# Gating six sums of b and forming M's blocks during the second f pass, with accumulating stores into the output

## The chip, the cores and the metric

The kernel runs on one core of one Trainium2 chip. Each core has a matrix engine (TensorE, PE below; its weight loads are shown apart as PEld), a vector engine (VectorE, DVE), a scalar engine (ScalarE, ACT), GpSimd (POOL) and SyncE (SP). In this kernel POOL and SP issue transfers and compute nothing that matters here. SP's transfers go through a hardware queue (q1 in the profile), POOL's through a software queue (q0); both use the core's 16 DMA engines. The metric is the time of one execution on the device in microseconds.

## The reference

Two layers read the same input x (2048 tokens, width 640) and are mixed by a gate for each token:

```python
x = A_x
g = _sigmoid((x * gate_w).sum(-1, keepdims=True))
a = _A_ref(x, A_wqkv, A_wo)
b = _B_ref(x, B_w_gate, B_w_up, B_w_down)
return g * a + (1 - g) * b
```

`_A_ref` is a linear attention with 32 heads of 20: q, k and v come from one product with `wqkv`, `phi` makes q and k positive, `kv` and `z` are sums over all tokens, and the output is `num / den` times `wo`. `_B_ref` is a gated unit with 1536 hidden columns: `(sigmoid(x Wg) * (x Wu)) Wd`.

## The kernel before

**Data.** The output is held transposed, `out_t` with 640 rows (five blocks `o` of 128) and 2048 columns of tokens (four groups `g` of 512). A product of float32 values is made of three matmuls (`mm3`, lines 406 to 408): each operand is split into a high part (ACT copies, line 419) and a low part (DVE subtracts, line 423), and high x high, high x low and low x high are added up in PSUM.

**Fewer products.** Many block products are made by a scheme for 2 x 2 blocks with seven products in place of eight, which needs sums and differences of blocks ahead of the products.

**Order of the work.** After `kv` and `z`, the matrix M (`kv` of each head times `wo`, 640 x 640, stored as `m_dram`) takes the place of both in the attention: a = (phi(q) M) / den. The gated unit goes over the tokens in two pairs of groups: first groups 2 and 3 (`pr` = 1), then groups 0 and 1 (`pr` = 0, the second pair). In each pair a loop `f_phase` runs over 12 blocks f of hidden columns, in seven steps s; at odd f from 3 on, a generator `down_pair` multiplies two finished hidden blocks by their down weights and adds the results into the tile `tb` (five o, two g). The down weights are loaded in three pieces into `wf` by `load_wf` (SP's queue, line 363). After both pairs come the attention products of groups 2 and 3 (eleven units with (0, 4) behind; `a_unit`, n counts them), and those of groups 0 and 1 (two `ABlock`s and two single units).

**What b becomes.** In the first pair, the ten sums of `tb` are stored into `b_dram`. Six of them, (o, g) = (0..3, 1), (1, 0) and (3, 0), are stored once; the other four are stored in two goes, the second an accumulating store. For the attention units of groups 2 and 3 all ten are loaded back as `bl` (`load_b`), multiplied by `omg`, which is 1 - g for each token (`load_omg`, `scale_b`), and added to the product by DVE (`finish`), which then goes to `out_t`. From the fourth unit on the product of `bl` and `omg` is first written to the PSUM bank (`queue_seed`), and PE adds its product to this seed; ACT copies the result (line 419) and SP stores it.

**M's blocks.** In the second pair's f, `queue_m` loads the rows of M as `mr`, splits them into `mt` and stores them as `mp_dram`, for the units. For the 2 x 2 scheme of groups 0 and 1, sums and differences of M's blocks are needed as well: `load_ms` loads raw rows ahead of f = 11 on POOL's queue (`mt`, then `mr` and `mv`, 16 loads of 80 KB), and `queue_ms` makes the sums (DVE, in two parts) and the splits into weights between the units, at about 689 to 704 us.

**The denominator** runs on the side: `pden` loads are summed by DVE into `fac` (line 427), stored as `den_dram`, loaded again with another layout, inverted and stored as `fac_dram`; SP loads that as `fac`, the factor by which DVE scales phi(q) (`pq_scale`).

**What sets the order.** Each engine works in program order. The order of ACT's and DVE's side work is set by a planner (`Order`): `order.add` queues a piece with its costs, `order.fill` puts queued pieces where its own model of the engines sees room, `order.need` forces one. Waits between engines come from the data. SP and POOL each issue their transfers in order; a POOL transfer takes one of eight slots in turn and waits until the transfer that had the slot has landed.

Of the kernel before, what the change touches and what calls it, by code (L numbers as in the profile page):

```python
# [7 lines left out]
F32 = mybir.dt.float32  # L8
# [365 lines left out]
def gated_mix_kernel(ctx: ExitStack, tc: tile.TileContext, xt, xn, wk, wv, wo, wst_q, wst_f, out_t):  # L374
# [70 lines left out]
    def add(out, a, b, after=""):  # L445
        vec2(out, a, b, OP.add, after)
# [12 lines left out]
    b_dram = dram.tile([P, KC, 2, TG], F32, name="b_dram")  # L459
    mp_dram = dram.tile([P, KC, 2, D], F32, name="mp_dram")  # L460
    gate_dram = dram.tile([2, S], F32, name="gate_dram")
    gate_rep = dram.tile([S // P, H, P], F32, name="gate_rep")
# [1260 lines left out]
    def queue_m(u=0):  # L1723
# [13 lines left out]
        order.add(a_cost(D), v_cost(D), fn, "m", lambda: order.when(raw) + DEN_LAG / 2, spare=True)  # L1737

    def m_close():
        nonlocal tb  # L1740
        mp_cm.__exit__(None, None, None)
        m1_cm.__exit__(None, None, None)
        kp_cm.__exit__(None, None, None)
        down_pool.append(ctx.enter_context(tc.tile_pool(name="down", bufs=1, reuse_waits="tile")))
        down_cms.append(tc.tile_pool(name="down1", bufs=1, reuse_waits="tile"))
        down_pool.append(down_cms[0].__enter__())
        tb = down_pool[0].tile([P, KC, 2, TG], F32, name="tb")
        sp.t = max(sp.t, order.act + A_LAG, order.vec + V_LAG, gp.cell[0])
        load_d()
        load_d()  # L1750
        for n in waiting_d:
            queue_d(n)
        other.append(Next(0, 1, xf, CW, c1_x, True))
# [142 lines left out]
    seen = set()  # L1896

    class DownPair:

# [269 lines left out]
    def f_phase(pr, q, hooks={}):  # L2169
# [67 lines left out]
        for f in range(FC):  # L2237
# [5 lines left out]
            if f % 2 and f > 1:  # L2243
                if pr:
                    pass
                elif f == FC - 3:
# [3 lines left out]
                    load_ms(0)  # L2250
                    load_ms(1)
                elif f == FC - 1:
                    load_m(0)
                down = down_pair(pr, f // 2 - 1)
# [118 lines left out]
    order.slack(False)  # L2373
    q = q_phase(0, lambda k: [tuple(t[:, k] for t in b12)], {0: [lambda: next(down), more_c], 1: [lambda: next(down)], 8: [lambda: order.need((nx[1], 6), False)], 9: [lambda: queue_ds(LAST), lambda: queue_df(LAST)], 10: [lambda: queue_last("T2", "T3", "T4")]})

    groups = (2, 3, 0, 1)
    PL, PQ, BL, OMG, MHL = {}, {}, {}, {}, {}

# [32 lines left out]
    def load_b(g):  # L2411

        if g < 2:
            BL[g] = [tb[:, o, g] for o in range(KC)]
        elif g == groups[0]:
            BL[g] = [ct("bl") for _ in range(KC)]
            for o in reversed(range(KC)):
                sp.dma_start(BL[g][o], b_dram[:, o, g - 2])
        else:
            t = [x3_tile("bl") for _ in range(2)]  # L2420
            sp.dma_start(t[0], b_dram[:, 0:3, g - 2])
            sp.dma_start(t[1][:, 0:2], b_dram[:, 3:5, g - 2])
            BL[g] = [t[o // 3][:, o % 3] for o in range(KC)]
        BL[g, "at"] = lambda: max(order.when(t) for t in BL[g])

    def load_omg(g):

        OMG[g] = down_pool[1].tile([P, TG], F32, name="omg", tag="omg") if g == groups[0] else tt("omg")
        sp.dma_start(OMG[g], gate_dram[1, g * TG:(g + 1) * TG].partition_broadcast(P))

# [30 lines left out]

    def finish(g, o, ps, c0, c1):
        dst = BL[g][o]
        add(dst[:, c0:c1], ps[:, c0:c1], dst[:, c0:c1], "p")
        sp.dma_start(out_t[o * P:(o + 1) * P, g * TG + c0:g * TG + c1], dst[:, c0:c1])

    PT, MS, MR = {}, {}, {}

    def load_ms(i):

        if i == 0:
            t = f32(down_pool[1].tile([P, 2, D], F32R, name="mt", tag="mt"))
            raw = [t[:, j] for j in range(2)]
        else:
            raw = [down_pool[1].tile([P, D], F32, name=n, tag=n) for n in ("mr", "mv")]
        for j in range(2):
            c0 = (2 * i + j) * P
            m_rows(raw[j].rearrange("p (k c) -> p k c", c=P), slice(c0, c0 + P), gp)
        MR[i] = raw, lambda: max(order.when(t) for t in raw)

    def queue_ms(i):

        raw, at = MR.pop(i)
        w = 2 * P
        g, v = raw
        a11, a12, a21, a22 = g[:, :w], g[:, w:2 * w], v[:, :w], v[:, w:2 * w]
        g5, v5 = g[:, 2 * w:], v[:, 2 * w:]

        def sums(part):
            if part == 0:  # L2490
                add(a22, a21, a22)
                sub(a21, a11, a21)
            else:
                sub(a11, a22, a11)
                sub(a12, a12, a11)
                sub(g5, g5, v5)

        def form(n, src):
            if i not in MS:
                t = ws_tile() if i == 0 else None  # L2500
                MS[i] = [t[:, c] for c in range(2)] if t is not None else \
                    [wg_tile().rearrange("p a b -> p (a b)")[:, :9 * P] for _ in range(2)]
            h, l = (t[:, n * w:n * w + width(src)] for t in MS[i])
            split(h, l, src)
        for part in range(2):
            order.add(0, 2 * v_cost(w), lambda part=part: sums(part), None, at)
        for n, t in enumerate((a22, a11, a21, a12, g5)):
            order.add(a_cost(width(t)), v_cost(width(t)), lambda n=n, t=t: form(n, t), ("ms", i))

# [25 lines left out]
    def a_first():  # L2535
# [15 lines left out]
    load_p(groups[1])  # L2551
    pq_tiles(groups[1])
    for g in groups[:2]:
        load_b(g)
    load_omg(groups[1])
    queue_scale(groups[1])
    queue_pq(groups[1])
    last_down(0, range(2 * KC))
# [20 lines left out]
    def a_unit(g, o, cuts=(0, TG), tag="rot", seed=False):  # L2579
# [4 lines left out]
        for c0, c1 in zip(cuts, cuts[1:]):  # L2584
# [3 lines left out]
            if seed and len(cuts) > 2:  # L2588
                dst = BL[g][o]
                ch = c0 + P if c1 == TG else c1  # L2590
                vec_copy(dst[:, c0:ch], ps[:, c0:ch], "p")
                if ch < c1:
                    act(dst[:, ch:c1], ps[:, ch:c1], AF.Copy, "p")
                    nc.scalar.dma_start(out_t[o * P:(o + 1) * P, g * TG + ch:g * TG + c1], dst[:, ch:c1])
                sp.dma_start(out_t[o * P:(o + 1) * P, g * TG + c0:g * TG + ch], dst[:, c0:ch])
                continue
            if seed:
# [3 lines left out]
                continue  # L2601
            order.need(("b", g, o))
            finish(g, o, ps, c0, c1)

# [5 lines left out]
    for n, (g, o) in enumerate(units[:-1]):  # L2610
# [3 lines left out]
        if n == 0:  # L2614
            queue_b_scale(g, range(3))
            queue_scale(groups[2])
            for m in groups[2:]:
                pq_tiles(m)
        elif o == 0:
# [3 lines left out]
            queue_t = queue_pt()  # L2623
            queue_ms(0)
        for i in range(3, 5) if n == 0 else (n + 4,) if n + 4 < len(units) else ():
# [10 lines left out]
    class ABlock(Block):  # L2636
# [39 lines left out]
        def s3(self):  # L2676
            order.need(("ms", self.i))
            order.need(("pt", 1))
# [38 lines left out]
    queue_t(3)  # L2717
    queue_ms(1)
    queue_b_scale(0, (1,))
# [6 lines left out]

    ahead = {(0, 2): ("ms", 0), (1, 1): ("pt", 0), (1, 2): ("pt", 2), (0, 4): ("pt", 3), (0, 7): ("ms", 1)}
    for i, s in [(i, s) for i in range(2) for s in (1, 2)] + [(i, s) for i in range(2) for s in (3, 4, 5, 7, 6)]:
# [45 lines left out]
```

## Time and profile before

| | |
|---|---|
| runs | 729.59 us median of 3 (729.37 to 731.28) |
| profiled execution | 728.96 us |
| its span in the trace | 727.1 us |
| granted TensorE clock | 1.00 |
| busy: PE, DVE, ACT, POOL | 99%, 78%, 50%, 16% of the span |

A row of the trace has the start in us, the duration, the engine, the line, the operation, the tiles as out<-in, the shape, and in brackets the idle time ahead of it with what ended it. "SPq", "ACTq" and "PEq" are an engine's own queue of instructions. In a row of a DMA the duration is that of the issue; how long a transfer took to land stands in a list of its own. A line is often that of a helper, so rows are told apart by their tiles.

### The profile page before, as it was taken

How to read it: one execution, taken by the hardware profiler on the slowest of the kernel's cores; microseconds unless marked ns; L12 is line 12 of the kernel's file. 1: busy time of each engine (PE TensorE's matmuls, PEld its weight loads, DVE VectorE, ACT ScalarE, POOL GpSimd, SP SyncE). 2: the span in 40 equal slices, each digit the busy share in tenths (PEclk: the TensorE clock that was granted, in tenths of full speed). 3: DMA queues.
4: the chain of work that ended last, by engine and by line, in shares of the span. 5: the costliest groups of instructions: out<-in, count | busy, mean ns of one | idle time of the engine just before them, and what ended most of it. 6: DMA issues, size and time to landing. Idle time of an engine off the chain costs nothing.

```text
span 727.1 us, 9849 instructions
## 1 busy us (share of the span) xinstructions
PE 723.0 (99%) x3424; PEld 610.7 (84%) x3424; DVE 568.3 (78%) x988; ACT 360.0 (50%) x673; POOL 118.6 (16%) x204
## 2 busy tenths in 40 slices
PE   9999999999999999999999999999999999999998
PEld 8999999888888888888888888888888888888887
DVE  4988877987687889898988884557667766689983
ACT  5764749267656653535455862354332232332551
POOL 0311111113312211211221133023011341000000
PEclk9999999999999999999999999999999999999999
DMA  8474558598787866557688779968979597859212
GB/s 280 109 200 114 174 133 266 135 325 300 278 309 258 330 238 232 188 212 258 244 333 319 187 254 366 342 227 253 345 250 360 182 306 193 315 219 355 79 67 102
DMA packets 63097, 175.23 MB, mean 241 GB/s; under 512 B 11803, under 2 KB 22955, under 8 KB 59463
## 3 DMA queue, kind: packets, MB, share of 16 engines
q1 hardware_dynamic: 43846, 104.29, 43.3%
q0 software_dynamic: 18912, 70.08, 27.8%
q8 instruction: 27, 0.44, 0.2%
q10 hardware_dynamic: 288, 0.23, 0.1%
q14 instruction: 24, 0.19, 0.1%
HBM read 104.62 MB, written 64.97 MB: 233 GB/s over the span
## 4 chain that ended last, share of the span: by engine, by line
PE 99%; DVE 0%; ACT 0%; issue 0%
PE ch L406 11%; PE ch L408 11%; PE ch L407 11%; PE cc L406 9%; PE cc L407 9%; PE cc L408 9%; PE dd L406 8%; PE dd L407 7%; PE dd L408 7%; PE rot L407 6%; PE rot L406 6%; PE rot L408 6%; PE rot L1560 1%; PE rot L496 0%; PE ch L980 0%; PE dd L980 0%
## 5 line engine op out<-in xcount | busy, mean ns | idle before, releaser
L419 ACT ACTIVATE c<-ch 128x512 f32<-128x512 f32 x49 | 29.3, 597 | 90.3 <-PE ch L408 87.4
L423 DVE TENSOR_TENSOR hf<-c,hf 128x512 fp32r<-128x512 f32 x77 | 52.5, 687 | 24.4 <-ACT hf L419 24.0
L419 ACT ACTIVATE hf<-c 128x512 fp32r<-128x512 f32 (+1 forms) x79 | 48.5, 624 | 37.8 <-DVE c L423 37.8
L423 DVE TENSOR_TENSOR c<-cc,c 128x512 f32<-128x512 f32 x38 | 26.2, 689 | 39.8 <-PE cc L408 24.1
L406 PE MATMUL ch<-xth,ws 128*128 128x512 f32 x112 | 43.8, 391 | 0.0
L408 PE MATMUL ch<-xth,ws 128*128 128x512 f32 x112 | 43.6, 390 | 0.0
L407 PE MATMUL ch<-xtl,ws 128*128 128x512 f32 x112 | 43.6, 390 | 0.0
L423 DVE TENSOR_TENSOR tb<-rot,tb 128x512 f32<-128x512 f32 x60 | 39.1, 682 | 2.6 <-PE rot L408 2.6
L423 DVE TENSOR_TENSOR tb<-dd,tb 128x512 f32<-128x512 f32 x41 | 28.1, 686 | 8.9 <-PE dd L408 8.9
L423 DVE TENSOR_TENSOR c<-c,c 128x512 f32<-128x512 f32 x48 | 33.0, 687 | 2.6 <-ACT c L419 2.0
L419 ACT ACTIVATE c<-dd 128x512 f32<-128x512 f32 x21 | 12.5, 597 | 41.5 <-PE dd L408 41.5
L406 PE MATMUL dd<-xrh,wg 128*128 128x512 f32 x84 | 32.9, 391 | 0.0
L407 PE MATMUL dd<-xrl,wg 128*128 128x512 f32 x84 | 32.7, 389 | 0.0
L407 PE MATMUL cc<-xbl,ws 128*128 128x512 f32 x84 | 32.7, 389 | 0.0
L408 PE MATMUL dd<-xrh,wg 128*128 128x512 f32 x84 | 32.7, 389 | 0.0
L406 PE MATMUL cc<-xbh,ws 128*128 128x512 f32 x84 | 32.7, 389 | 0.0
L408 PE MATMUL cc<-xbh,ws 128*128 128x512 f32 x84 | 32.7, 389 | 0.0
L419 ACT ACTIVATE dd<-ch 128x512 f32<-128x512 f32 x22 | 12.8, 583 | 34.0 <-PE ch L408 34.0
L423 DVE TENSOR_TENSOR wst<-wst 128x256 f32<-128x256 f32 (+2 forms) x69 | 27.4, 412 | 1.4
L408 PEld LDWEIGHTS ch<-xth,ws 128*128 128x128 f32 x112 | 21.0, 188 | 4.7 <-DVE ws L423 0.3
L407 PEld LDWEIGHTS ch<-xtl,ws 128*128 128x128 f32 x112 | 21.0, 188 | 4.3
L406 PEld LDWEIGHTS ch<-xth,ws 128*128 128x128 f32 x112 | 21.0, 188 | 4.1
(720 smaller groups left out, 2334.1 us busy)
## 6 DMA issues: line engine op xcount, KB each, us to landing
wf<-ws POOLq DMA_DIRECT2D x12, 1152.0 KB, 7.6
ws<-wf SPq DMA_DIRECT2D x11, 1152.0 KB, 9.3
wst<-wst_f SPq DMA_DIRECT2D x12, 640.0 KB, 4.8
wf<-wg POOLq DMA_DIRECT2D x12, 640.0 KB, 6.8
wd<-wd POOLq DMA_DIRECT2D x12, 640.0 KB, 8.2
wg<-wf SPq DMA_DIRECT2D x12, 640.0 KB, 5.5
wf<-wd SPq DMA_DIRECT2D x10, 640.0 KB, 11.1
xnst<-xn SPq DMA_DIRECT2D x16, 320.0 KB, 4.6
```

The costliest lines, as they stand in the source:

```text
L406: nc.tensor.matmul(out, l_hi, r_hi, start=first, stop=False, skip_group_check=True)
L407: nc.tensor.matmul(out, l_hi, r_lo, start=False, stop=False, skip_group_check=True)
L408: nc.tensor.matmul(out, l_lo, r_hi, start=False, stop=last, skip_group_check=True)
L419: nc.scalar.activation(out, src, fn, **kw)
L423: nc.vector.tensor_tensor(out, a, b, op=op)
L1560: nc.tensor.matmul(ps[:w, :w], v[:, m, :w], gt[:, m, c0:c0 + w], start=(m == 0), stop=(m == KC - 1))
```

## The change

It has four parts.

1. **Gated b.** In the first pair, the six sums that were stored once into `b_dram` are multiplied by `omg` on DVE (`queue_gate`) and stored straight into `out_t` on POOL's queue. `omg` of groups 2 and 3 is loaded early into two `wst` tiles (`early_omg`). Of the ten `bl` loads four are left.
2. **Last products by accumulating stores.** The units of these six are no longer added to by DVE: ACT copies the product into a tile `st`, and POOL's queue adds it to `out_t` by an accumulating store. Seeds are left for units n = 2, 4 and 9; unit 0 is still added by DVE.
3. **M's sums in f.** `queue_ms` moves into the second pair's f, at (7, 4) and (9, 3). It loads the raw rows (`mr`, `mv`, eight loads for each of two groups), makes sums and splits there and stores the weights as `ms_dram` (six stores). `load_ms` later loads them as finished weights, on SP's queue.
4. **The last half unit.** It is copied by ACT in one piece of 256 columns and stored in one piece, in place of a DVE copy and an ACT copy of 128 each.

With these, `omg` is no longer loaded in f, and `load_omg` and `load_b` stand elsewhere.

```diff
+    def queue_ms(i):
+        raw = [down_pool[1].tile([P, D], F32, name=n, tag=n) for n in ("mr", "mv")]
+        for j in range(2):
+            c0 = (2 * i + j) * P
+            m_rows(raw[j].rearrange("p (k c) -> p k c", c=P), slice(c0, c0 + P), gp)
...
+        def forms(c0, srcs):
...
+                t = down_pool[1].tile([P, 2, D], F32R, name="mt", tag="mt")
+                c = 0
+                for src in srcs:
+                    split(t[:, 0, c:c + width(src)], t[:, 1, c:c + width(src)], src)
+                    c += width(src)
+
+                def rest():
+                    gp.dma_start(ms_dram[i, :, :, c0:c0 + n], f32(t[:, :, :n]))
+                    free[0] = gp.cell
+                order.then(rest)
+            order.add(a_cost(n), v_cost(n), fn, "ms", lambda: free[0][0] + DEN_LAG / 2, spare=True)
+        for part in range(2):
+            order.add(0, 2 * v_cost(w), lambda part=part: sums(part), "ms", landed, spare=True)
+        forms(0, (a22, a11))
+        forms(2 * w, (a21, a12))
+        forms(4 * w, (g5,))
...
+    def queue_gate(o, g):
+        dst = tb[:, o, g]
+        def gate():
+            vec2(dst, dst, OMG[g + 2], OP.mult)
+            gp.dma_start(out_t[o * P:(o + 1) * P, (g + 2) * TG:(g + 3) * TG], dst)
+        order.add(0, v_cost(TG), gate, ("gate", o, g), lambda: order.when(OMG[g + 2]))
...
-                gp.dma_start(b_dram[:, o, g], dst, accum_op=OP.add if apart and p == LAST else OP.bypass)
+                if apart:
+                    gp.dma_start(b_dram[:, o, g], dst, accum_op=OP.add if p == LAST else OP.bypass)
+                else:
+                    queue_gate(o, g)
...
         if i == 0:
-            t = f32(down_pool[1].tile([P, 2, D], F32R, name="mt", tag="mt"))
-            raw = [t[:, j] for j in range(2)]
+            t = ws_tile()
+            sp.dma_start(f32(t), ms_dram[0])
+            MS[0] = [t[:, c] for c in range(2)]
...
+        (1, 2): [lambda: [order.need(("gate", o, g)) for o, g in ((1, 1), (3, 1), (0, 1), (2, 1), (1, 0), (3, 0))]],
         (2, 7): [queue_m],
-        (FC - 2, 2): [lambda: load_wd(FC - 2), lambda: load_omg(groups[0])],
+        (7, 4): [lambda: queue_ms(0)],
+        (9, 3): [lambda: queue_ms(1)],
+        (FC - 2, 2): [lambda: load_wd(FC - 2)],
...
-                dst = BL[g][o]
-                ch = c0 + P if c1 == TG else c1
-                vec_copy(dst[:, c0:ch], ps[:, c0:ch], "p")
-                if ch < c1:
-                    act(dst[:, ch:c1], ps[:, ch:c1], AF.Copy, "p")
-                    nc.scalar.dma_start(out_t[o * P:(o + 1) * P, g * TG + ch:g * TG + c1], dst[:, ch:c1])
-                sp.dma_start(out_t[o * P:(o + 1) * P, g * TG + c0:g * TG + ch], dst[:, c0:ch])
+                dst, queue = BL[g][o], nc.scalar if c0 else sp
+                act(dst[:, c0:c1], ps[:, c0:c1], AF.Copy, "p")
+                queue.dma_start(out_t[o * P:(o + 1) * P, g * TG + c0:g * TG + c1], dst[:, c0:c1])
                 continue
...
-            order.need(("b", g, o))
-            finish(g, o, ps, c0, c1)
+            if n == 0:
+                order.need(("b", g, o))
+                add(BL[g][o], ps, BL[g][o], "p")
+                sp.dma_start(out_t[o * P:(o + 1) * P, g * TG:(g + 1) * TG], BL[g][o])
+                continue
+            dst = ct("st")
+            act(dst, ps, AF.Copy, "p")
+            gp.dma_start(out_t[o * P:(o + 1) * P, g * TG:(g + 1) * TG], dst, accum_op=OP.add)
...
-        a_unit(g, o, tag=("rot", "dd", "cc", "ch")[n % 4], seed=n > 2)
+        a_unit(g, o, tag=("rot", "dd", "cc", "ch")[n % 4], seed=n in (2, 4, 9))
```

How the rows move on the engines, first POOL's queue in the second pair's f, from the `pden` loads of the second half of the denominators on. Before:

```order
L363 DMA pden<-p_dram 128x512 x10
L363 DMA den_dram<-fac 128x512 x2
L363 DMA fac<-den_dram 32x4x128 x8
L363 DMA fac_dram<-fac 128x128
L363 DMA mt<-m_dram 32x5x128 x8
L363 DMA mr<-m_dram 32x5x128 x4
L363 DMA mv<-m_dram 32x5x128 x4
L363 DMA fac_dram<-fac 128x128
```

The same stretch of the changed kernel:

```order
L363 DMA pden<-p_dram 128x512 x8
L363 DMA mr<-m_dram 32x5x128 x4
L363 DMA mv<-m_dram 32x5x128 x4
L363 DMA pden<-p_dram 128x512 x2
L363 DMA den_dram<-fac 128x512 x2
L363 DMA ms_dram<-mt 256x1x512
L363 DMA fac<-den_dram 32x4x128 x8
L363 DMA ms_dram<-mt 256x1x512
L363 DMA mr<-m_dram 32x5x128 x4
L363 DMA mv<-m_dram 32x5x128 x4
L363 DMA ms_dram<-mt 256x1x128
L363 DMA ms_dram<-mt 256x1x512
```

The first group of raw rows stands ahead of the last two `pden` loads, an `ms_dram` store behind the `den_dram` stores and another ahead of the second group; the 16 loads behind `fac_dram` are gone.

Next DVE in the down products of f = 9 (tiles `dd`, `cc`, `rot` are PSUM banks, `tb` the sums of b). Before:

```order
L423 TENSOR_TENSOR tb<-dd_5626,tb 128x512
L423 TENSOR_TENSOR tb<-cc_5631,tb 128x512
L423 TENSOR_TENSOR tb<-rot_5558,tb 128x512
L423 TENSOR_TENSOR tb<-rot_5564,tb 128x512
L423 TENSOR_TENSOR fac<-fac 128x256
L423 TENSOR_TENSOR fac<-fac 128x128
```

The same place in the changed kernel:

```order
L423 TENSOR_TENSOR tb<-dd_5653,tb 128x512
L423 TENSOR_TENSOR tb<-cc_5658,tb 128x512
L423 TENSOR_TENSOR mv<-mv 128x256
L423 TENSOR_TENSOR mv<-mr,mv 128x256
L423 TENSOR_TENSOR tb<-rot_5581,tb 128x512
L423 TENSOR_TENSOR tb<-rot_5587,tb 128x512
```

Two sums of M's second group stand ahead of the two `tb<-rot`, and the sums of `fac` have moved behind.

Last DVE ahead of the attention units (`pl` and `wu` hold phi(q), `pq` its low parts, `bl` is b). Before:

```order
L423 TENSOR_TENSOR tb<-dd_6046,tb 128x512
L423 TENSOR_TENSOR pq<-pl,pq 128x512 x3
L423 TENSOR_TENSOR tb<-dd_6068,tb 128x512
L423 TENSOR_TENSOR pq<-pl,pq 128x512
L423 TENSOR_TENSOR pq<-wu,pq 128x512
L427 SCALAR_TENSOR_TENSOR pl<-pl,fac 128x512
L423 TENSOR_TENSOR tb<-dd_6089,tb 128x512
L427 SCALAR_TENSOR_TENSOR pl<-pl,fac 128x512 x4
L423 TENSOR_TENSOR pq<-pl,pq 128x512 x5
L423 TENSOR_TENSOR bl<-bl,omg 128x512
L423 TENSOR_TENSOR bl<-rot_6127,bl 128x512
L423 TENSOR_TENSOR bl<-bl,omg 128x512
```

The same place in the changed kernel:

```order
L427 SCALAR_TENSOR_TENSOR wu<-wu,fac 128x512
L423 TENSOR_TENSOR pq<-pl,pq 128x512 x2
L423 TENSOR_TENSOR tb<-dd_6113,tb 128x512
L423 TENSOR_TENSOR pq<-pl,pq 128x512 x2
L423 TENSOR_TENSOR pq<-wu,pq 128x512
L427 SCALAR_TENSOR_TENSOR pl<-pl,fac 128x512
L423 TENSOR_TENSOR tb<-dd_6134,tb 128x512
L427 SCALAR_TENSOR_TENSOR pl<-pl,fac 128x512 x4
L423 TENSOR_TENSOR pq<-pl,pq 128x512 x5
L423 TENSOR_TENSOR bl<-bl,omg 128x512
L423 TENSOR_TENSOR bl<-rot_6174,bl 128x512
L423 TENSOR_TENSOR cc_6223<-bl,omg 128x512
```

The scale of `wu` stands in this stretch, with one more `pq` behind the first `tb<-dd`, and the third unit's seed (`cc<-bl,omg`) where the second unit's scale stood.

More of the change, by code (lines that the diff above doesn't have):

```diff
@@ L2414, in load_b @@
             BL[g] = [tb[:, o, g] for o in range(KC)]
[L2415 to L2418, printed above, removed]
-        else:
[L2420 to L2429, printed above, removed]
+        else:
+            BL[g] = {o: ct("bl") for o in ((0, 2, 4), (4,))[g - 2]}
+            for o, t in BL[g].items():
+                sp.dma_start(t, b_dram[:, o, g - 2])
+        BL[g, "at"] = lambda: max(order.when(t) for t in (BL[g].values() if g > 1 else BL[g]))
     def pq_scale(g, u):
@@ L2460, in scale_b @@
         vec2(BL[g][o], BL[g][o], OMG[g], OP.mult)
-    def finish(g, o, ps, c0, c1):
-        dst = BL[g][o]
-        add(dst[:, c0:c1], ps[:, c0:c1], dst[:, c0:c1], "p")
-        sp.dma_start(out_t[o * P:(o + 1) * P, g * TG + c0:g * TG + c1], dst[:, c0:c1])
-    PT, MS, MR = {}, {}, {}
+    PT, MS = {}, {}
     def load_ms(i):
         if i == 0:
-            t = f32(down_pool[1].tile([P, 2, D], F32R, name="mt", tag="mt"))
-            raw = [t[:, j] for j in range(2)]
-        else:
[L2475 to L2508, printed above, removed]
+            t = ws_tile()
+            sp.dma_start(f32(t), ms_dram[0])
+            MS[0] = [t[:, c] for c in range(2)]
+        else:
+            MS[1] = [wg_tile().rearrange("p a b -> p (a b)")[:, :9 * P] for _ in range(2)]
+            for c in range(2):
+                sp.dma_start(f32(MS[1][c]), ms_dram[1, :, c])
     def queue_pt():
```

55 lines of the change are left out of this document (39 added, 16 removed).

## The prediction

> **What bounds the kernel now.** I read the page first: busy shares (engine, busy time, share of the span, instructions), then the chain that ended last.
>
> ```profile
> PE 723.0 (99%) x3424; PEld 610.7 (84%) x3424; DVE 568.3 (78%) x988; ACT 360.0 (50%) x673; POOL 118.6 (16%) x204
> ...
> PE 99%; DVE 0%; ACT 0%; issue 0%
> ```
>
> TensorE (PE) is busy 723.0 of 727.1 us and the chain is PE throughout. A busy PE can still hide stalls, so next come PE's waits, and then windows around the places that the change touches (busy time of PE, PEld, DVE, ACT, POOL, then granted clock, DMA share, GB/s).
>
> ```profile
> PE rot L496 <- PEq L2765: 0.8, 1, 0.8
> ```
> ```profile
> 540.00:544.00 4.00, 4.00 (x19) 3.30 (x19) 2.62 (x5) 2.10 (x4) 0.00 (x0) 1.00 1.02 412
> 560.00:564.00 4.00, 4.00 (x19) 3.30 (x19) 2.89 (x5) 0.60 (x1) 0.00 (x0) 1.00 0.41 157
> 572.00:576.00 4.00, 4.00 (x19) 3.30 (x19) 1.76 (x3) 0.60 (x1) 2.13 (x4) 1.00 0.83 222
> 584.00:588.00 4.00, 4.00 (x20) 3.30 (x19) 2.70 (x6) 0.60 (x1) 1.31 (x3) 1.00 1.05 297
> 600.00:604.00 4.00, 4.00 (x19) 3.32 (x18) 3.90 (x9) 0.58 (x1) 2.26 (x4) 1.00 1.12 193
> ```
>
> PE's only wait is 0.8 us at the start; in each window it is busy 4.00 of 4 us at clock 1.00. The change leaves PE's instructions and their order as they are. So nothing on PE is saved, work taken from DVE or the queues is worth nothing by itself, and the change can only make PE wait, or shorten the microseconds behind the last matmul. The question is which margins it eats. The windows show where transfers have none: the DMA engines are full (share over 1.0) around 584 and 600 us.
>
> **The change part by part.** Costs are made against the profiled execution, 728.96 us (span 727.1 and 1.86 outside it). The median of the three runs, 729.59, is 0.63 above it; the sum is added to that median. A measurement of this kernel can tell about 0.3%, 2.2 us, from no change.
>
> *The down weights of f = 9.* POOL's queue first, then SP's row with the weight load `wf` (three pieces), then PEld's first use of it.
>
> ```profile
> 570.12 0.55 POOL L363 DMA_DIRECT2D den_dram<-fac  x1 [5.04 <-DVE fac L427]
> 573.37 0.55 POOL L363 DMA_DIRECT2D den_dram<-fac  x1 [2.71 <-DVE fac L427]
> 574.42 2.20 POOL L363 DMA_DIRECT2D fac<-den_dram  x4 [0.50 <-issue]
> 579.59 2.17 POOL L363 DMA_DIRECT2D fac<-den_dram  x4 [2.97 <-PE ch L408]
> ...
> 587.24 3.99 POOL L363 DMA_DIRECT2D mt<-m_dram  x7
> ```
> ```profile
> 575.12 1.87 SPq L363 DMA_DIRECT2D wf<-wd  x3
> ```
> ```profile
> 587.93 0.19 PEld L406 LDWEIGHTS dd<-hf,wf 128*128 128x128 f32 x1
> ```
>
> The transfers between 573 and 588, and below them those of the cycle of f = 7, 536 to 551 (issues: count, KB, us to landing):
>
> ```profile
> DMA packets 1440, 4.44 MB, mean 296 GB/s; under 512 B 238, under 2 KB 366, under 8 KB 1312
> ...
> q0 software_dynamic: 338, 0.79, 18.4%
> ...
> wf<-wd SPq DMA_DIRECT2D x2, 640.0 KB, 12.8
> ```
> ```profile
> DMA packets 1430, 5.32 MB, mean 355 GB/s; under 512 B 158, under 2 KB 158, under 8 KB 1300
> ...
> q0 software_dynamic: 464, 1.70, 28.4%
> ...
> wf<-wd SPq DMA_DIRECT2D x2, 640.0 KB, 12.8
> ```
>
> The first piece of `wf` is issued at 575.12 and takes 12.8 us, to 587.92; PEld uses it at 587.93. The margin is nothing. The changed kernel puts two things ahead of it on POOL's queue (q0). The first `den_dram` store, whose last DVE sum now stands behind two sums of M, moves from 570.12 to about where the second was, 573.2: 0.26 MB that used to go before SP's queue filled the engines. And the first `ms_dram` store (256 rows of 512 floats, 0.52 MB) goes behind the second. That is 0.79 MB more. At the 412 GB/s of 540 to 544 it takes 1.9 us, at the 296 of this stretch 2.7; I take 2.3, between them. Against it: 572 to 576 has a share of 0.83, so 0.7 us are free; and the second four `fac` loads wait for the later `den_dram` store, so about half of their 0.26 MB falls behind `wf`, 0.4 us. Net 1.2 us of waiting on PE, bounds 0 and 2.7. The zero end has a row: from 536 to 551 POOL's queue moved 1.70 MB, twice as much, `wf` took the same 12.8 us, and PE did not wait. I stay off it because that stretch moved 355 GB/s and this one 296, with more packets under 512 bytes. The Trainium skill ("DMA: Bandwidth & Descriptors", Specifications) gives the fabric 435 GB/s; by that figure the 0.79 MB take 1.8 us and 0.7 would be left, an estimate; no window here reaches that rate.
>
> *M's second group.* Its eight loads `mr`, `mv` stand behind the second `ms_dram` store, and DVE's sum `mv<-mv`, behind `tb<-cc`, waits for the last of them, with two `tb<-rot` queued behind it. The landing of a `den_dram` store (573.37), of before's first two m loads and of its eighth (592.27), then DVE and PE at that place:
>
> ```profile
> den_dram<-fac POOLq DMA_DIRECT2D x1, 256.0 KB, 5.6
> ```
> ```profile
> mt<-m_dram POOLq DMA_DIRECT2D x2, 80.0 KB, 6.3
> ```
> ```profile
> 592.27 0.57 POOL L363 DMA_DIRECT2D mt<-m_dram  x1 [1.04 <-DMA fac_dram<-fac]
> ...
> 600.87 1.14 POOL L363 DMA_DIRECT2D mv<-m_dram  x2 [0.32 <-DMA mt<-m_dram]
> ```
> ```profile
> mt<-m_dram POOLq DMA_DIRECT2D x1, 80.0 KB, 10.6
> ```
> ```profile
> 600.23 0.68 DVE L423 TENSOR_TENSOR tb<-cc,tb 128x512 f32<-128x512 f32 x1
> 600.82 1.28 DVE L423 TENSOR_TENSOR tb<-rot,tb 128x512 f32<-128x512 f32 x2
> ```
> ```profile
> 603.12 0.39 PE L406 MATMUL rot<-hf,wf 128*128 128x512 f32 x1
> ```
>
> The store takes the place of the m loads at 587.24, and by the 5.6 us of the `den_dram` store lands near 593. The last `mv` load waits for its queue slot until then; with 6.3 to 10.6 us it lands between 599.3 and 603.6. I take 600, near the short end: eight m loads fewer stand behind it, and SP's four `fac` loads that went beside it come later. DVE gets there at 600.8; the first `tb<-rot` takes 0.7 behind two half-width sums of 0.4, so PE's `rot` at 603.12 is kept up to a landing at 601.6 (602.8 if PE is 1.2 late already). Cost 0; the far bound is 603.6 less 601.6, 2.0 us.
>
> *The seed of the third unit.* It is no longer added after the product but seeded before it.
>
> ```profile
> 657.04 0.69 DVE L423 TENSOR_TENSOR tb<-dd,tb 128x512 f32<-128x512 f32 x1 [0.23 <-PE dd L408]
> 657.64 2.48 DVE L427 SCALAR_TENSOR_TENSOR pl<-pl,fac 128x512 f32<-128x512 f32 x4
> 660.05 3.09 DVE L423 TENSOR_TENSOR pq<-pl,pq 128x512 fp32r<-128x512 f32 x5
> 663.06 0.69 DVE L423 TENSOR_TENSOR bl<-bl,omg 128x512 f32<-128x512 f32 x1
> 663.85 0.69 DVE L423 TENSOR_TENSOR bl<-rot,bl 128x512 f32<-128x512 f32 x1
> 664.46 0.68 DVE L423 TENSOR_TENSOR bl<-bl,omg 128x512 f32<-128x512 f32 x1
> ```
> ```profile
> 665.00 0.39 PE L406 MATMUL cc<-pq,ws 128*128 128x512 f32 x1
> ```
>
> DVE runs without a gap from 657.04, and one scale (`wu<-wu,fac`, 0.6) has moved into this run. Of it 0.23 goes into the wait ahead of 657.04 and 0.2 into that ahead of 663.85. The seed takes the place of the scale at 664.46, 0.2 later, and ends at 665.3; PE wants it at 665.00. Cost 0.3 us, bounds 0 and 0.6 (the scale whole).
>
> *Behind the last matmul.* DVE's 128 columns, then ACT's, become one ACT copy of 256.
>
> ```profile
> 723.87 0.29 DVE L810 COPY tb<-rot 128x128 f32<-128x128 f32 x1 [1.37 <-PE rot L408]
> ...
> 724.19 0.28 ACT L419 ACTIVATE tb<-rot 128x128 f32<-128x128 f32 x1 [7.39 <-DVE tb L810]
> 724.50 0.35 ACTq L2594 DMA_DIRECT2D out_t<-tb  x1
> ```
>
> ACT waited for DVE; alone it starts at 723.9 and, with twice the columns, issues 0.1 to 0.2 earlier. The store is twice as large. I take 0.1 us gained (bounds 0.2 gained, 0.1 lost).
>
> *At no cost:* the six gating products and their stores (the stores they replace are as large); M's first group, loaded in the half-empty stretch (0.41 at 560 to 564); the later `fac` and `omg` loads, covered by f's last products; the `ms_dram` loads, covered by a unit's products and more; the accumulating stores, whose landing only frees tiles; the dropped sums, which PE did not wait for. If a cover is gone, it shows as a wait of PE of that name, of the DMA's remainder.
>
> Sum: 1.2 + 0 + 0.3 - 0.1 = 1.4. From 728.96 that is 730.4; on the median 731.0.
>
> **The rivals.**
> 1. *Nothing waits.* The added packets go beside `wf` as at 536 to 551, and the seed is just in time: -0.1, so 729.5. Against it: a margin of 0.01 us in a full stretch.
> 2. *M's rows too late, a slower kernel.* What stands ahead on POOL's queue slides by the same 1.2 as `wf`: the store lands at 594.1, the last load takes 10.6 as the eighth did, 604.7, and DVE holds both `tb<-rot`. It decides from a landing at 602.8 on, so costs 1.9: 732.9. For it: 600 to 604 has share 1.12 at 193 GB/s.
> A mechanism of its own would lead there too: DVE's work holding up POOL's issues. DVE is busy 3.90 of 4 us at 600 to 604, and two issues there take 1.14, 0.57 each, as the seven from 587.24 do. If each of the group's eight were held for one DVE operation of 0.68, they would land 5.4 later, at 605.4, and cost 2.6: 733.6. The Trainium skill ("SBUF — State Buffer", "Who interferes with whom") has such a lock between DVE's two-port modes and GpSimd; the issue times here do not show it.
> 3. *`wf` late by the whole bound.* 2.7 instead of 1.2: 732.5.
> 4. *More is gained than the tail.* With PE busy 4.00 of 4 in every window I see no 2.2 us to gain.
>
> **How the numbers follow.** Forecast 731.0, 0.42; rival 1, 0.15; rival 2, 0.18, and with the lock 0.05; rival 3, 0.17; rival 4, 0.03. Same ends at 729.59 + 2.2 = 731.8: the forecast and rival 1 lie below, rivals 2 and 3 above. So same 0.57, slower 0.40, faster 0.03. The range goes from 729.3 (rival 1 and the 0.2 by which the lowest run lies below the median) to 733.6 (rivals 2 and 3 with the lock); both ends' remainders and rival 4 are left out.
>
> **What would show it.** Right: the only new waits of PE over 0.2 us are about 1.2 at `dd<-hf,wf` near 588, behind the `wf` load, and 0.3 at `cc<-pq` near 666, behind DVE; none near 604; ACT's last copy directly behind PE. Wrong: no wait at `wf`; or a wait at `rot<-hf,wf` near 604 behind DVE's `tb`; or one that I put at no cost.

## The result and the profile after

| | before | after |
|---|---|---|
| median of 6 runs, same chip | 729.54 us (729.25 to 731.28) | 733.97 us (733.04 to 735.29) |
| ratio, 95% interval | | 1.0058 [1.0042, 1.0073] |
| span of the profiled execution | 727.1 us | 731.5 us |
| granted TensorE clock | 1.00 | 1.00 |

The changed kernel is slower by 4.4 us, three times the 1.4 that I had added up, and 0.4 above the upper end of the range. First the page of after: busy shares, and the chain that ended last by engine.

```profile
PE 723.7 (99%) x3424; PEld 610.2 (83%) x3424; DVE 567.0 (78%) x984; ACT 361.9 (49%) x676; POOL 128.1 (18%) x216
...
PE 94%; DMA 3%; DVE 2%; POOL 1%; issue 0%; SPq 0%; ACT 0%; DVEq 0%
```

PE's busy time has grown by 0.7 us only, and its count of instructions is the same. But the chain is no longer PE alone: 6% of it runs through DMA, DVE and POOL. What PE waits for (total, times, longest):

```profile
PE rot L406 <- DVE tb L423: 1.7, 1, 1.7
PE dd L406 <- DMA wf<-wd: 1.3, 1, 1.3
PE rot L497 <- PEq L2795: 0.8, 1, 0.8
PE cc L406 <- DVE cc L423: 0.3, 1, 0.3
```

Before had only the third. The three new ones are where the prediction looked: the down weights of f = 9, M's second group, the third unit's seed. Their places, from PE's timeline of after (start, duration; the last row is the last matmul):

```profile
587.87 0.50 PE L406 MATMUL dd<-hf,wf 128*128 128x512 f32 x1
...
589.85 0.39 PE L408 MATMUL rot<-hf,wf 128*128 128x512 f32 x1
591.55 0.47 PE L406 MATMUL dd<-hf,wf 128*128 128x512 f32 x1 [1.31 <-DMA wf<-wd]
...
606.40 0.50 PE L406 MATMUL rot<-hf,wf 128*128 128x512 f32 x1 [1.68 <-DVE tb L423]
...
668.89 0.50 PE L406 MATMUL cc<-pq,ws 128*128 128x512 f32 x1 [0.33 <-DVE cc L423]
...
727.59 0.28 PE L408 MATMUL rot<-hf,wf 128*128 128x256 f32 x1
```

The two `dd` and the last matmul in before:

```profile
588.16 0.39 PE L406 MATMUL dd<-hf,wf 128*128 128x512 f32 x1
...
590.20 0.39 PE L406 MATMUL dd<-hf,wf 128*128 128x512 f32 x1
...
723.55 0.28 PE L408 MATMUL rot<-hf,wf 128*128 128x256 f32 x1
```

The same matmul in both traces gives a running account (the starts of `rot` and `cc` before, 603.12 and 665.00, stand in the prediction):

| matmul | before | after | difference | new since the row above |
|---|---|---|---|---|
| first `dd` with the new `wf` | 588.16 | 587.87 | -0.29 | -0.29 (already there at 177 us; the first 200 us differ by up to 1.3 us between executions) |
| second `dd` | 590.20 | 591.55 | +1.35 | +1.64 |
| `rot` | 603.12 | 606.40 | +3.28 | +1.93 |
| `cc` | 665.00 | 668.89 | +3.89 | +0.61 |
| last | 723.55 | 727.59 | +4.04 | +0.15 |
| end of the span | 727.10 | 731.45 | +4.35 | +0.31 |

So the three waits make 4.2 us and 0.3 lie behind the last matmul; the other two rows, -0.29 and +0.15, nearly cancel. A wait costs more than the idle time in its row: that counts from the end of the matmul before it (589.85 + 0.39 = 590.24), while the next would have started 0.23 after its start, at 590.08. So the second `dd` is 1.47 late, not 1.31. And the first matmul behind a wait is itself slower, 0.47 to 0.50 in place of 0.39, which puts off the next by some 0.1.

The largest wait, read backwards from `rot`, is in the chain of after from 587 to 607 us (start, us, what):

```profile
575.41 16.00 DMA wf<-wd
...
597.20 0.29 DVE mt L423
597.50 0.28 issue
597.78 2.30 POOL mr L363 x4
600.08 1.69 POOL mv L363 x3
601.77 3.06 DMA mv<-m_dram
...
605.32 0.42 DVE mv L423
605.74 0.61 DVE tb L423
...
606.40 0.50 PE rot L406
```

Its first row is the second piece of `wf`, behind the wait at 591.55, 16 us under way: it landed at 591.41. In before the same piece landed at 589.53 (read from the updates of its semaphore in the packed trace), and PEld first used it at 590.06. So the change made it 1.9 us later, and about 0.5 of that was margin. PE's `rot` waits for DVE's `tb`, which stands behind two sums of M (`mv`), which wait for a load, which POOL issued only at 601.77, because the first of its eight waited for DVE's `mt` at 597.20. POOL's queue and ACT's and DVE's rows at that place:

```profile
573.18 0.55 POOL L363 DMA_DIRECT2D den_dram<-fac  x1 [7.18 <-DVE fac L427]
574.84 0.55 POOL L363 DMA_DIRECT2D den_dram<-fac  x1 [1.11 <-DVE fac L427]
575.51 0.69 POOL L363 DMA_DIRECT2D ms_dram<-mt  x1
...
586.82 0.69 POOL L363 DMA_DIRECT2D ms_dram<-mt  x1 [0.15 <-issue]
597.78 2.30 POOL L363 DMA_DIRECT2D mr<-m_dram  x4 [10.28 <-DVE mt L423]
600.07 2.28 POOL L363 DMA_DIRECT2D mv<-m_dram  x4
```
```profile
595.27 0.31 ACT L419 ACTIVATE mt<-mr 128x128 fp32r<-128x128 f32 x1 [2.35 <-DMA ms_dram<-mt]
```
```profile
596.60 0.69 DVE L423 TENSOR_TENSOR tb<-ch,tb 128x512 f32<-128x512 f32 x1
597.20 0.28 DVE L423 TENSOR_TENSOR mt<-mr,mt 128x128 fp32r<-128x128 f32 x1
...
604.86 0.42 DVE L423 TENSOR_TENSOR mv<-mv 128x256 f32<-128x256 f32 x1 [2.51 <-DMA mv<-m_dram]
```

POOL sat 10.28 us with nothing to issue. The second group is loaded into the same `mr` and `mv` that hold the first, and the last piece of the first (128 columns, `forms(4 * w, (g5,))`) is still to be split from `mr` into `mt`: a write after a read. That split in turn needs `mt` back from the second `ms_dram` store (issued at 586.82, landed 8.4 later) on ACT, and on DVE its place behind `tb<-ch`. The store took long, the loads themselves were quick (issues from 587 to 605: count, KB, us to landing; then the stretch 600 to 604: busy times, clock, DMA share, GB/s):

```profile
ms_dram<-mt POOLq DMA_DIRECT2D x1, 512.0 KB, 8.4
mr<-m_dram POOLq DMA_DIRECT2D x4, 80.0 KB, 4.8
mv<-m_dram POOLq DMA_DIRECT2D x4, 80.0 KB, 3.6
```
```profile
600.00:604.00 4.00, 4.00 (x19) 3.31 (x18) 2.35 (x4) 0.00 (x0) 2.99 (x6) 1.00 0.59 143
```

The DMA engines, full there before (share 1.12), are at 0.59. The loads were issued while the share fell from 0.83 (596 to 600) to this.

### The profile page after: what moved, and what is told of

Its sections match the earlier page's. It is cut to its first block, busy times and chain, and to the rows that moved or that the text cites. A ratio compares the mean times of both kernels' runs of the same rounds, so it can differ in the third digit from the quotient of the medians.

```text
span 731.5 us, 9873 instructions
## 1 busy us (share of the span) xinstructions
PE 723.7 (99%) x3424; PEld 610.2 (83%) x3424; DVE 567.0 (78%) x984; ACT 361.9 (49%) x676; POOL 128.1 (18%) x216
## 4 chain that ended last, share of the span: by engine, by line
PE 94%; DMA 3%; DVE 2%; POOL 1%; issue 0%; SPq 0%; ACT 0%; DVEq 0%
PE ch L406 10%; PE ch L408 10%; PE ch L407 10%; PE cc L406 8%; PE cc L408 8%; PE cc L407 8%; PE dd L406 7%; PE dd L407 7%; PE dd L408 7%; PE rot L406 5%; PE rot L407 5%; PE rot L408 5%; DMA wf<-wd 2%; PE rot L1561 1%; DVE pq L423 1%; PE rot L497 0%
```

## The experiments

All are edits of the changed kernel. The base is the kernel before on the same chip; after's own ratio is 1.0058.

**M's part undone.** The old `queue_ms` and `load_ms` are put back in their old places; gating, accumulating stores and the tail stay.

```diff
-                elif f == FC - 1:
+                elif f == FC - 3:
...
+                    load_ms(0)
+                    load_ms(1)
...
-        (7, 4): [lambda: queue_ms(0)],
-        (9, 3): [lambda: queue_ms(1)],
```

> M's part of the change is undone: raw rows loaded ahead of f = 11 and summed late, as before; the gated sums, accumulating stores, seeds and the one-piece last store stay. Theory (the two long waits of PE, 1.3 behind the wf load and 1.7 behind DVE's tb, come from M's part alone; 0.3 at the seed and some 0.4 behind the last matmul come from the rest): both long waits vanish, the 0.3 stays, span about 728 (731.5 less 3.6), median about 730.3. Rival (the gated stores and later loads of the other part share the cause): at least one of the two waits stays, and the median is 732 or more.

Measured: 729.84 us (728.95 to 731.49, 12 runs), ratio 1.0004 [0.9994, 1.0014]. Neither long wait is there: none at `rot` and none over 0.2 us at 590. (The profiled execution, 731.49, has waits of 0.7 and 0.8 for `ws` and `wf` at 513 to 519 us, where POOL and SP issue the same transfers as in before; the median lies 1.65 below it. The trace of the third experiment has such waits there too and the other ten have none, so they seem to come and go between executions.) So M's part alone makes the change slow, and the other three together cost less than can be told. One thing came out otherwise than expected: the 0.3 at the seed is gone as well, though the third unit is still seeded. DVE's scale `wu<-wu,fac` stands at 642.26 here, as in before (642.34), and at 655.61 in after. So that wait takes both the seed and the scale that comes into this stretch with M's part.

**The last split in a tile of its own.** It no longer needs `mt` back from a store; its place in DVE's order is the same.

```diff
-                t = down_pool[1].tile([P, 2, D], F32R, name="mt", tag="mt")
+                t = down_pool[1].tile([P, 2, P], F32R, name="mf", tag="mf") if n == P else \
+                    down_pool[1].tile([P, 2, D], F32R, name="mt", tag="mt")
```

> The small last quarter of M's group is split into a tile of its own, so that its split no longer waits until the second ms_dram store has landed (595.2); nothing moves in any engine's order. Theory (the eight loads of the second group wait for DVE's low split of that quarter, which stands behind tb<-ch in DVE's order and is reached at 597.2 whatever the store does): the first mr load is still issued at 597.5 to 598, PE's wait at rot<-hf,wf stays within 0.3 of 1.7, the median near 734. Rival (the landing of the store holds the chain): the loads go 2 us earlier, the wait falls under 0.3, the median near 732.2.

Measured: 734.64 us (734.04 to 736.45, 4 runs), 1.0070 [1.0052, 1.0087]. POOL's queue and DVE in its trace:

```profile
599.18 2.30 POOL L363 DMA_DIRECT2D mr<-m_dram  x4 [10.21 <-DVE mf L423]
```
```profile
598.60 0.28 DVE L423 TENSOR_TENSOR mf<-mr,mf 128x128 fp32r<-128x128 f32 x1
```

PE runs 1.3 us later here than in after, and so do these rows: nothing has moved. It is not the store's landing but the place of the split in DVE's order, behind `tb<-ch` as before, that sets the loads.

**The last split earlier.** Own tile again, and queued ahead of the split of the second half (the sums are kept where they were by a later due time).

```diff
         forms(0, (a22, a11))
+        forms(4 * w, (g5,))
         forms(2 * w, (a21, a12))
-        forms(4 * w, (g5,))
...
```

> As the one with the tile of its own, and the quarter's split is queued right behind the first two, ahead of the second ms_dram store; the second group's sums keep their place in DVE's order. Theory (the wait for the raw tiles holds the loads): the mr loads are issued from about 587 on instead of 597.8, land before 601, and PE's wait of 1.7 at rot<-hf,wf is gone: median about 732.2; the 1.3 at the wf load stays or changes by under 0.5. Rival (the full DMA engines hold M's rows, not the wait): the loads take 10 us and more beside wf, wg and ws, land after 603, and the wait stays over 1.

Measured: 734.43 us (732.62 to 734.81, 4 runs), 1.0058 [1.0040, 1.0075]. A miss: the loads left at 595.56, not where I had put them, since the split that is now last also reads `mr` and `mv`, and had slid behind on ACT and DVE:

```profile
595.56 2.30 POOL L363 DMA_DIRECT2D mr<-m_dram  x4 [6.21 <-DVE mt L423]
```

The wait at `rot` fell from 1.7 to 0.9 us; two waits for `wf`, 2.2 us together, one of them at 518 where the program is as before, took its place in the total. The write after read had only found its next reader. Whether loads issued at 588 would have landed in time in the full stretch, the question of the prediction, stays open; so does a run in which the second group has raw tiles of its own, which was not made.

**The first `ms_dram` store taken away from the weight load.** It is left out at 575 and written later with other data, so M's first weights are wrong.

```diff
+                    if not i and not c0:
+                        free[0] = [order.vec + 8.0]
+                        return
                     gp.dma_start(ms_dram[i, :, :, c0:c0 + n], f32(t[:, :, :n]))
+                    if i and c0 == 2 * w:
+                        gp.dma_start(ms_dram[0, :, :, :n], f32(t[:, :, :n]))
```

> The first ms_dram store (0.52 MB at 575.5) is left out there and its place in ms_dram is filled later, near 613, from another tile, so M's first weights are not the right values. Theory (these bytes ahead of wf's second piece made it late by 1.9): the second piece lands 1.2 to 1.9 us earlier, PE's wait of 1.3 at dd<-hf,wf falls under 0.3, the median about 732.5, with the 1.7 at rot<-hf,wf as it was or up to 1.3 longer, since PE comes there earlier and the mr loads do not. Rival (the later den_dram stores and fac loads, not the store, hold wf): the wait stays over 1.

Measured: 735.01 us (731.93 to 735.11, 5 runs), 1.0059 [1.0040, 1.0078]. PE's waits, and its windows behind the longest:

```profile
PE rot L406 <- DVE tb L423: 2.4, 1, 2.4
...
PE cc L406 <- DVE cc L423: 0.3, 1, 0.3
...
```
```profile
604.00:608.00 4.00, 1.59 (x8) 1.12 (x7) 2.85 (x6) 0.19 (x1) 0.00 (x0) 1.00 0.18 51
608.00:612.00 4.00, 4.00 (x12) 3.13 (x11) 3.15 (x7) 0.79 (x2) 0.00 (x0) 0.57 0.00 0
608.20:611.50 3.30, 3.30 (x9) 2.58 (x8) 2.94 (x7) 0.29 (x1) 0.00 (x0) 0.50 0.00 0
```

The wait for `wf` is gone, as the theory says; but PE, no longer held there, waits 2.4 at `rot`, and behind that wait the granted clock is 0.57 for one window, and 0.50 inside it: 12 matmuls where 19 are usual, another 1.5 us. Four of the five runs have a mean granted clock of 0.998 and took 734.55 to 735.11; the fifth, at 1.000, took 731.93. So the median holds a slow stretch beside the store's price, and the list of waits tells that the store alone, without the later `den_dram` stores, made the wait for `wf`.

**The second group's sums later in DVE's order.** Eight us more in the due time of the second group (i = 1): the sums stand behind the `tb` that PE waits for.

```diff
-            return max(order.when(t) for t in raw) + DEN_LAG / 2
+            return max(order.when(t) for t in raw) + DEN_LAG / 2 + 8 * i
```

> Only the place of M's second group's sums is moved: in DVE's order they stand some ten rows later, behind the tb sums of the f = 9 pair, in place of ahead of two of them. Loads and stores stay as they are. Theory (PE's wait of 1.7 at rot<-hf,wf is DVE standing in front of the raw rows, with the tb sums queued behind): that wait is gone though the mr loads are still issued near 598, the 1.3 at the wf load and the 0.3 at the seed stay, median 1.8 lower than the changed kernel, about 732.5. Rival (DVE is late for another reason, or the next operation takes the wait over): a wait over 1 us stays between 603 and 612.

Measured: 731.59 us (730.31 to 732.96, 12 runs), 1.0028 [1.0020, 1.0037]. Its POOL queue, DVE, and PE's waits:

```profile
596.87 2.30 POOL L363 DMA_DIRECT2D mr<-m_dram  x4 [9.61 <-DVE mt L423]
```
```profile
601.35 1.28 DVE L423 TENSOR_TENSOR tb<-rot,tb 128x512 f32<-128x512 f32 x2
...
607.51 0.42 DVE L423 TENSOR_TENSOR mv<-mv 128x256 f32<-128x256 f32 x1
```
```profile
PE dd L406 <- ACT ch L419: 0.6, 1, 0.6
PE cc L406 <- DVE cc L423: 0.3, 1, 0.3
```

The loads wait for the split nearly as long as in after, and PE does not notice: the two `tb<-rot` go ahead of the sums. (The 0.6 at `dd` is the place of the wait for `wf`, at 590.60; here the list puts it down to ACT.) One number in the order is worth 2.4 us by the medians (733.97 less 731.59) and 2.2 by the ratios (1.0058 and 1.0028). By the account 1.9 of it is the wait at `rot`; the rest was not forecast, and the wait for `wf`, 0.6 here and 1.3 in after, is not the same in each trace: 0.6 to 1.3 in the six that have it at the second piece.

**The old tail.** DVE copies 128 columns and ACT 128, in two stores, as before.

```diff
-                dst, queue = BL[g][o], nc.scalar if c0 else sp
-                act(dst[:, c0:c1], ps[:, c0:c1], AF.Copy, "p")
+                ch = c0 + P if c1 == TG else c1
+                vec_copy(dst[:, c0:ch], ps[:, c0:ch], "p")
...
```

> The last half unit is copied and stored as before (DVE 256 and 128 columns, ACT 128, two stores of 64 KB behind the last matmul); all else is the changed kernel. Theory (the one store of 128 KB lands later than one of 64 KB, 3.2 against 2.6 us, more than ACT's earlier start gives back): from the start of the last matmul to the end of the span 3.5 to 3.6 us, as before, in place of 3.9. Rival (the 0.4 is scatter of single executions): 3.8 to 4.0.

Measured in one run: 733.95 us. From the start of the last matmul to the end of the span are 3.84 us (728.35 to 732.19), which the theory did not expect; after has 3.86, the kernel before 3.55, and M's part undone, with the new tail, 3.55 too. So the edit of the tail is worth 0.02 us at most: ACT issues its store 0.73 us after the start of the last matmul instead of 0.95, and the larger store takes as much longer. In all twelve traces the last transfer lands 2.63 to 2.69 us after that start. The 0.3 lies behind the landing. There SP goes through a fixed row of waits for the semaphores of the transfers, and these of them stand behind the last landing (before, M's part undone, after; count and times):

```profile
L2770 SPq EVENT_SEMAPHORE  x3: 17/17/28, 726.2 to 727.0; - x3
L2785 SPq EVENT_SEMAPHORE  x3: 17/17/28, 728.9 to 729.7; - x3
L2800 SPq EVENT_SEMAPHORE  x8: 17/28/28, 730.3 to 731.4; - x8
```

One takes 0.06 us, so five more make 0.3. Transfers take the semaphores in turn. In before, the last store has number 109, the last in SP's row; in after it has 102, and SP still has to ask for the rest. The ten traces with M's part in f have the 0.3, the two without it do not. That the number follows from the count of SP's transfers, which M's part changes, is argued and not tested.

**The third unit not seeded.** Unit n = 2 is added to by DVE again.

```diff
-        a_unit(g, o, tag=("rot", "dd", "cc", "ch")[n % 4], seed=n in (2, 4, 9))
+        a_unit(g, o, tag=("rot", "dd", "cc", "ch")[n % 4], seed=n in (4, 9))
...
```

> The third unit (n = 2) is not seeded but added by DVE after its product, as before; all else is the changed kernel. Theory (PE waits for the seed): the wait of 0.3 at cc<-pq near 668, and the slower matmuls behind it, are gone, and no other takes its place near 671. Rival (DVE is late by the same amount for the next unit): a wait of 0.2 or more within the next two units.

Measured in one run: 732.12 us. The wait at `cc` is gone and no other has come among the units; 1.6 at `rot` and 1.2 at `dd` remain. The seed's term stands, with the condition that the first experiment showed.

**All four places repaired at once.** Sums and splits of the first group behind the `fac` loads, the second group at (9, 7), no seed for n = 2, the old tail.

```diff
-        (9, 3): [lambda: queue_ms(1)],
+        (9, 7): [lambda: queue_ms(1)],
...
-            return max(order.when(t) for t in raw) + DEN_LAG / 2
+            return max(order.when(t) for t in raw) + DEN_LAG / 2 + (6, 4)[i]
...
```

> All parts of the change are kept but placed apart from the four losses: the sums and stores of M's first group follow the fac loads, its second group is loaded only behind them near 615, the third unit is not seeded, the last half unit is copied as before. Theory (the losses are waits of these four places and nothing else): no wait of PE over 0.3 us from 560 on, median within 0.7 of before, 729.0 to 730.4, and not below it by more than the scatter, since PE has nothing to gain. Rival (accumulating stores, or added traffic as such, cost something too): 731 or more with waits elsewhere.

Measured: 731.00 us (730.07 to 733.32, 11 runs), 1.0025 [1.0014, 1.0036]. A miss, and the wait that is left is in another place:

```profile
627.94 0.50 PE L406 MATMUL dd<-hf,wf 128*128 128x512 f32 x1 [1.44 <-DMA wf<-wd]
```

Nothing waits at 590; but the second group's loads, issued from 613.34 on, now lie beside the `wf` load of f = 11, which holds PE by 1.4.

**Later sums and no seed.** The edits of the fifth and the seventh run together.

```diff
+            return max(order.when(t) for t in raw) + DEN_LAG / 2 + 8*i
...
+        a_unit(g, o, tag=("rot", "dd", "cc", "ch")[n % 4], seed=n in (4, 9))
```

> Two repairs together: the sums of M's second group later in DVE's order, and the third unit not seeded. The theory has three separate waits of PE, each with the two slowed matmuls behind it: about 1.9 us at rot<-hf,wf, 1.3 to 1.6 at the second piece of wf, 0.5 at cc<-pq. Two of them go, the one at wf stays: 4.4 - 1.9 - 0.5 = 2.0 above the kernel before at most, 1.2 at least, so a ratio of 1.0016 to 1.0027 and one wait of 0.6 to 1.3 at dd<-hf,wf in the profile. Rival, the waits hide one another (PE that was not held at one place is held more at the next): the time stays at 1.003 or above, and the wait at wf grows to 2 us.

Measured: 730.81 us (729.32 to 732.44, 12 runs), 1.0017 [1.0008, 1.0025]. Besides the one at the start, one wait:

```profile
PE dd L406 <- DMA wf<-wd: 0.8, 1, 0.8
```

Here the waits add up: the two that were taken away came off the time, and the 1.29 us left above the kernel before (730.81 less 729.52) are nearly the 0.8 of this wait, the 0.3 that a wait costs beside its idle time, and the 0.3 at the end of the span.

**The first group earlier.** As the run before, with M's first group at (6, 2) and the second at (9, 4): nothing of M but the small third store (0.13 MB) lies beside the `wf` load of f = 9.

```diff
-        (7, 4): [lambda: queue_ms(0)],
-        (9, 3): [lambda: queue_ms(1)],
+        (6, 2): [lambda: queue_ms(0)],
+        (9, 4): [lambda: queue_ms(1)],
```

> As the run before it, and M's first group is loaded one step row earlier ((6, 2) in place of (7, 4)), so that its three stores lie between the pden loads ahead of the den_dram stores and no longer beside the weight load wf of f = 9; the second group is loaded one step later ((9, 4)), behind all fac loads. Theory: what held wf was the 0.79 MB ahead of it on POOL's queue, so the wait at wf goes to 0 to 0.3 us and the time to the kernel before's, ratio 0.9995 to 1.001. Rival (as undoing all showed): the stretch has no free place, and the bytes hold another wf load, that of f = 7 or f = 11, by 0.8 to 1.4 us: ratio 1.0012 to 1.0025.

Measured: 733.19 us (732.05 to 735.54, 6 runs), 1.0056 [1.0041, 1.0071]. The rival, and more of it. POOL's queue and PE:

```profile
537.11 1.20 POOL L363 DMA_DIRECT2D mr<-m_dram  x2 [0.31 <-DMA wu<-wf]
...
539.74 1.70 POOL L363 DMA_DIRECT2D mv<-m_dram  x3
```
```profile
553.23 0.50 PE L406 MATMUL dd<-hf,wf 128*128 128x512 f32 x1 [1.64 <-DMA wf<-wd]
...
556.81 0.47 PE L406 MATMUL dd<-hf,wf 128*128 128x512 f32 x1 [1.24 <-DMA wf<-wd]
```

There is no wait at 590, 604 or 668; the eight 80 KB loads (0.66 MB) now lie beside the `wf` load of f = 7 and hold it at two pieces, 2.9 us. So in each of the three cycles in which 0.5 MB or more of the bytes that the change moved were issued ahead of the last piece of a `wf` load, f = 7, 9 and 11, PE waited for that load. The 16 loads of before, which the change moved, held nothing: they start at 587.24, when the first piece of `wf` has all but landed (587.89) and the second is 2.3 us from it. It is no rule for every cycle: at f = 5 all the kernels have a 640 KB store (`mp_dram`) and 320 KB of loads (`mr`) of M ahead of the last piece of `wf` (from 500 us on), and ten of the twelve traces have no wait there.

## Why the prediction was wrong, point by point

- **PE has nothing to gain:** held. Its work and clock are the same, and no kernel of the experiments has a median below that of the kernel before.
- **The down weights, 1.2 us:** the size held nearly (1.31 idle, 1.6 in the account), and so did the moves on POOL's queue (573.2 forecast for the first `den_dram` store, 573.18 found). The place was off by one piece. I looked at the first piece only, where the margin is 0.01; there the change cost 0.1 (the first matmul took 0.50 in place of 0.39). The second landed at 591.41 by the chain (575.41 + 16.00), when PE had stood ready since 590.1; its margin of about 0.5 I had not read. It came 1.9 later than in before, more than the 1.2 forecast, and the margin took the difference back: that the size came so near is in part luck. That M's bytes cause the wait is shown by the runs without them there, in which no such wait is left at 590, and by the two in which it moved with them to f = 11 and f = 7. The zero end, which I had from f = 7's cycle at 1.70 MB without a wait, is no rule: 0.66 MB on top of that cycle cost 2.9.
- **M's second group, no cost. This is the step that failed.** "The last `mv` load waits for its queue slot until then; with 6.3 to 10.6 us it lands between 599.3 and 603.6. I take 600." I took the queue's slots for the only thing that could hold the loads, and asked how full the engines were. The runs put another wait in its place: the loads overwrite tiles that the first group's last split still reads, and that split stands late in DVE's order. They left at 597.78 in place of about 588 to 593, and landed fast, in 3.6 to 4.8. The cost was 1.9 us where I had 0; that the far bound of 2.0 is so near is luck, since it came from slow loads. A second reading was wrong in the same step: I gave the `ms_dram` store the 5.6 us of a `den_dram` store of half its size, and it took 8.4, to 595.2; the run with a tile of its own shows that this did not decide. The wait was there to be seen: the code loads both groups under the tags `mr` and `mv`, and in DVE's order the last split of `mr` stands behind `tb<-ch`.
- **Rival 2** gave the right place and, at 604.7 against 604.84, the right landing, by luck: no load took 10.6 us, and the stretch was at 0.59 of the engines, not full. Its lock between DVE and POOL's issues is not there either: 0.57 us for each issue as before.
- **The seed, 0.3:** held at 0.33 of idle time, 0.6 in the account, and by the mechanism given: it takes the scale of `wu` in this stretch of DVE's rows.
- **The tail, -0.1:** 0.31 longer. The edit itself is worth 0.00 and 0.02, by the two pairs with and without it; the rest is five more of SP's closing waits behind the last landing, which the prediction has no term for.
- **The sum and the range:** two more things were left out. The sum has no term for what a wait costs beside its idle time, about 0.3 each (0.16 ahead of it, 0.1 behind). And the range took the unknown costs one at a time: rival 2 at 732.9 is 1.2 + 1.9 + 0.3 - 0.1 above the median of before. Measured were 1.6, 1.9, 0.6 and 0.3 at once, and 733.97 lies beyond 733.6.

## What to carry to other kernels

When loads move to an earlier place, ask first what still reads the tiles that they overwrite, and where that reader stands in its engine's order; how full the DMA engines are comes second. Work that may wait for a transfer belongs behind, not ahead of, what the bounding engine waits for on the same in-order engine: moving two small sums by a few rows was worth about 2 us. And where a stream of loads is just in time, bytes added beside it cost time, so the margin is to be read for each of its pieces; the place that cost nothing here was behind the landing of its first piece.

## What the runs showed of the hardware

- The clock: after 2.41 us without a matmul (604.24 to 606.65, with the first `ms_dram` store taken away) the granted clock was 0.57 from 608 to 612; in the packed trace's record of the clock it is 0.50 from 608.17 to 611.58, so it fell 1.5 us after PE was back and stayed low for 3.4. In the profiled execution of after, with waits of 1.68 and 1.31 us, it stayed at 1.00. The Trainium skill ("TensorE: Matmul & The Clock Gate", Part 1: The HAM clock gate) has the clock halved after an idle window of about 3.4 us. The one run here agrees with the half and not with the length: 2.41 us were enough.
- The first matmul behind a wait took 0.47 to 0.50 us instead of 0.39, even after a wait of 0.33.
- A 512 KB store took 8.4 us to land where the DMA engines are full (share 1.04 from 586.8 to 595.2), while 80 KB loads took 3.6 to 4.8 where the share fell from 0.83 to 0.59.
- The first 200 us differ by up to 1.3 us between the twelve traces, whose kernels are the same there, and 1.0 of it lies in the first 20 us; so effects of one us are better read from waits at their place than from one run's time.
